# One output transfer, or four on two queues, at the end of a decode kernel

## The chip, the cores and the metric

The kernel runs on one core of a Trainium2 chip. The metric is device time in microseconds (us), from runs on the chip; the lower the better. Beside it there is a profile of one execution, whose span reaches from the first to the last recorded instruction.

## The reference

One decode step of two branches that share a layer norm. Four batch rows of width 576 go in, four rows of 576 come out, in bfloat16.

```
xn  = layernorm(x)                                  # x: [4, 1, 576]
# A: attention over the last 2048 positions of a cache (32 query heads, 16 kv heads, head width 128)
q   = (xn @ wq) as heads
p   = softmax(q . k[window] * 128**-0.5)
a   = (p . v[window]) as one row @ wo
# B: an MLP mixer; with one position its shifted part hs is zero
h2  = gelu(layernorm(xn) @ w3) @ w4
out = x + a + (xn + h2)
```

## The kernel before

Nearly all of the work is reading: 87 MB of cache and weights go once through SBUF. SyncE issues all of these loads from one DMA queue, in the order of the program; each waits until the buffer that it fills has been released. ScalarE's DMA queue carries one transfer, the input `x_bf` (line 98), at the start: four rows of 1152 bytes.

The stages follow each other: the q projection; the scores over eight blocks of K, with the MLP's first product between them; the softmax (line 306 on); then sixteen heads of V, each with its sum, its selection and its part of the output projection; and last the remaining part of `w4`, loaded into `w_end` by five transfers (lines 558 and 559).

In the last stage the result comes together in the PSUM tile `ACC3`. It holds the output cut into four quarter rows of `DQ` = 144 columns: quarter q lies on the partitions from 32q, and of those 32 partitions every eighth (`NB` = 8) holds one of the four batch rows. So 16 partitions, 0, 8, 16 and so on to 120, hold the 16 runs of 144 numbers, 288 bytes each. `quad_out` (line 501) adds the products of `w4` into it, lines 569 to 573 the sums of the two other accumulators, and lines 574 and 575 the last parts of `w4` as their loads land. Then VectorE copies `ACC3` to the SBUF tile `fin` (line 579), and SyncE issues the store (line 580). Its source steps over partitions 0 to 127 by 8; on the side of the output its pattern has three dimensions, quarter, row and column.

After the store the program ends. The closing code, which the profile puts on line 606, is on every engine: SyncE waits for the semaphores of all DMA slots and of the other engines, in five instructions with two semaphores each and one more, and then all engines meet in barriers. Each transfer has one of eight semaphores, which go round; a transfer also waits until the one before it that used the same semaphore has landed. In the list of the closing waits each instruction names two: slots 3 and 2, then 4 and 1, 5 and 0, 6 and VectorE's, 7 and ScalarE's.

Of the kernel before, what the change touches and what calls it, by code (L numbers as in the profile page):

```python
# [20 lines left out]
def kernel(  # L21
# [19 lines left out]
    nc = tc.nc  # L41
    P = 128
# [8 lines left out]
    G = 32  # L51
# [18 lines left out]
    o2 = out.flatten_outer_dims()  # L70
# [289 lines left out]
    NB = B * rep  # L360
# [129 lines left out]
    DQ = D // 4  # L490
# [86 lines left out]

    fin = const.tile([P, DQ], out.dtype)
    nc.vector.tensor_copy(out=fin[:], in_=ACC3[:, 0:DQ])
    nc.sync.dma_start(out=o2.rearrange("b (q n) -> q b n", q=4), in_=fin[0:P:NB, :])  # L580


# [28 lines left out]
```

## Time and profile before

| what | us |
|---|---|
| median of three runs | 213.44 (213.19 to 213.72) |
| span of the profiled execution | 212.0 (212.03 to two places) |
| VectorE busy | 128.2 (60% of the span) |
| TensorE matmul busy | 98.4 (46%) |
| ScalarE busy | 17.4 (8%) |
| read from HBM | 87.17 MB, 411 GB/s over the span |
| the output store, issue on SyncE | 0.69, from 209.20 |

The profiled execution's own time is its span and what lies around it before the first and after the last instruction; the three runs were timed without such a breakdown. SyncE's and ScalarE's DMA-issuing instructions are not counted as busy, but the timeline shows them as SPq and ACTq with the time that issuing took on the engine's sequencer. The transfer itself runs later, on DMA engines. In the DMA view q1 is SyncE's queue and q10 ScalarE's.

### The profile page before, as it was taken

The numbers are of one execution on the slowest core, as the hardware profiler recorded it, in microseconds if no ns is written. First come the engines' busy times: TensorE is split into PE (matmuls) and PEld (weight loads), VectorE is DVE, ScalarE is ACT, GpSimd is POOL, SyncE is SP. The second block draws the span as 40 slices with busy tenths as digits, with TensorE's granted clock in tenths as the row PEclk, the third lists the DMA queues.
The fourth block names the chain that finished last, engine by engine and source line by source line (L and its number), as shares of the span: only waits on it lengthen the run. The fifth ranks groups of instructions, "written<-read, shape, count | busy, mean of one in ns | idle before, by whom it ended". The sixth has DMA issues, their size and how long they took to land. (4 is left out here: it accounts for less than half of the span.)

```text
span 212.0 us, 2539 instructions
## 1 busy us (share of the span) xinstructions
PE 98.4 (46%) x1071; PEld 50.5 (24%) x1071; DVE 128.2 (60%) x225; ACT 17.4 (8%) x35; POOL 1.8 (1%) x8
## 2 busy tenths in 40 slices
PE   1442059429903333423333421968573644555573
PEld 0111027408301011101111101734231321212241
DVE  7812592095349898979699916968475322145240
ACT  0004100000000000000000058730000000000000
POOL 2100000000000000000000000000000000000000
PEclk9999999999999999999999999999787555555555
DMA  7999999999999999999999999999999999999980
GB/s 261 427 457 433 411 442 454 392 420 460 420 420 457 411 445 433 408 451 399 433 427 420 436 415 432 436 423 423 426 430 417 434 415 438 423 427 419 423 356 18
DMA packets 5943, 87.32 MB, mean 412 GB/s; under 512 B 681, under 2 KB 685, under 8 KB 1453
## 3 DMA queue, kind: packets, MB, share of 16 engines
q1 hardware_dynamic: 5924, 87.17, 96.8%
q8 instruction: 8, 0.13, 0.3%
q14 instruction: 3, 0.02, 0.0%
q10 hardware_dynamic: 8, 0.00, 0.0%
HBM read 87.17 MB, written 0.00 MB: 411 GB/s over the span
## 5 line engine op out<-in xcount | busy, mean ns | idle before, releaser
L297 DVE STREAM_TRANSPOSE kt<-k 128x2048 int32<-128x2048 int32 x32 | 71.0, 2278 | 17.5 <-DMA k<-in_A_k_cache_dram 17.5
L304 PE MATMUL S<-kt,qz 128*32 128x512 bf16 x256 | 30.4, 622 | 56.9 <-DVE kt L297 56.9
L384 PE MATMUL O<-v,PZ 128*32 128x512 bf16 x256 | 23.6, 506 | 15.1 <-DMA v<-in_A_v_cache_dram 15.1
L304 PEld LDWEIGHTS <-qz 128*32 128x32 bf16 x256 | 9.5, 127 | 74.0 <-issue 67.5
L413 DVE TENSOR_SCALAR osum<-O,diag 128x128 f32<-128x128 f32 x16 | 5.6, 348 | 28.8 <-PE O L384 28.8
L415 DVE SCALAR_TENSOR_TENSOR osum<-O,diag,osum 128x128 f32<-128x128 f32 x48 | 16.5, 345 | 0.9
L384 PEld LDWEIGHTS <-PZ 128*32 128x32 bf16 x256 | 7.5, 116 | 22.5 <-DMA v<-in_A_v_cache_dram 12.6
L346 PE MATMUL pt<-ident,prs 128*128 128x128 bf16 x64 | 6.5, 287 | 10.1 <-DVE prs L342 10.1
L321 ACT ACTIVATE E<-S,nb 128x256 f32<-128x256 f32 x8 | 4.5, 704 | 69.9 <-DVE nb L318 69.9
L425 PEld LDWEIGHTS OT<-sel,osum 128*128 128x128 f32 x32 | 6.6, 258 | 13.5 <-issue 7.1
L425 PE MATMUL OT<-sel,osum 128*128 128x8 f32 x32 | 8.1, 326 | 3.4 <-DVE osum L415 3.4
L395 PE MATMUL ACC<-wo,onx 128*4 128x288 bf16 x64 | 4.5, 434 | 8.7 <-DVE onx L444 8.7
L346 PEld LDWEIGHTS <-prs 128*128 128x128 bf16 x64 | 5.8, 131 | 11.5 <-ACT prs L340 9.4
L342 DVE TENSOR_SCALAR prs<-E,rdm 128x512 bf16<-128x512 f32 x12 | 7.8, 801 | 0.0
L465 PEld LDWEIGHTS <-w3a 128*128 128x128 bf16 x108 | 6.9, 161 | 1.7 <-issue 1.7
L465 PE MATMUL ACC<-ln2T,w3a 128*128 128x4 bf16 x108 | 7.0, 202 | 0.0
L316 DVE TENSOR_REDUCE mx<-S 128x1 f32<-128x512 f32 x4 | 2.7, 681 | 5.4 <-PE S L304 5.4
L236 PE MATMUL qp<-wq,xnT 128*8 128x512 bf16 x32 | 3.8, 621 | 4.5 <-DMA wq<-in_A_wq_dram 4.5
L567 ACT COPY sums<-ACC 64x288 f32<-64x288 f32 x1 | 0.4, 393 | 64.5 <-PE ACC L395 64.5
L251 DVE CAST q_rows<-qp 128x256 bf16<-128x256 f32 x4 | 1.5, 420 | 5.9 <-PE qp L236 3.9
L340 ACT ACTIVATE prs<-E,rdm 128x512 bf16<-128x512 f32 x4 | 4.9, 1404 | 0.8 <-DVE rdm L328 0.8
L465 PEld LDWEIGHTS <-w3b 128*128 128x128 bf16 x72 | 4.5, 160 | 0.8 <-issue 0.8
(91 smaller groups left out, 68.1 us busy)
## 6 DMA issues: line engine op xcount, KB each, us to landing
v<-in_A_v_cache_dram SPq DMA_DIRECT2D x16, 2048.0 KB, 26.4
k<-in_A_k_cache_dram SPq DMA_DIRECT2D x7, 4096.0 KB, 30.6
wo<-in_A_wo_dram SPq DMA_DIRECT2D x4, 1152.0 KB, 29.8
wq<-in_A_wq_dram SPq DMA_DIRECT2D x2, 2048.0 KB, 12.9
k<-in_A_k_cache_dram SPq DMA_DIRECT2D x2, 2048.0 KB, 25.0
w3a<-in_B_w_dram SPq DMA_DIRECT2D x1, 2304.0 KB, 27.0
w3b<-in_B_w_dram SPq DMA_DIRECT2D x1, 2304.0 KB
w3b<-in_B_w_dram SPq DMA_DIRECT2D x1, 1728.0 KB, 34.6
```

The costliest lines, as they stand in the source:

```text
L297: nc.vector.transpose(out=ap32(kt[e], c0 * 2 * G, [[2 * G, C2 // 2], [1, 2], [2, G]]), in_=ap32(kn, c0 * 4 * G + e * G, [[4 * G, C2 // 2], ...
L304: nc.tensor.matmul(out=S[kq][c:c + 32, :].rearrange("p (c q l) -> p c q l", q=4, l=2), lhsT=qz[:, bp, m, y, :], rhs=kt[e][:, :, 4 * m:4 * ...
L321: nc.scalar.activation(out=E[:, :, g, x:GK:2].rearrange("p (c l) q -> p c q l", l=2), in_=S[g][:, 256 * x:256 * (x + 1)].rearrange("p (c q ...
L340: nc.scalar.mul(out=dst, in_=src, mul=rdm[:, b:b + 1])
L342: nc.vector.tensor_scalar_mul(out=dst, in0=src, scalar1=rdm[:, b:b + 1])
L346: nc.tensor.transpose(out=tp[:, cc, :], in_=pr[:, half * HC + cc, :, :, :].rearrange("p g k b -> p (g k b)"), identity=ident[:])
L384: nc.tensor.matmul(out=bank[G * j:G * j + G, :], lhsT=PZ[:, hp, c0:c0 + NI, :].rearrange("p c m -> p (c m)"), rhs=vn[:, c0:c0 + NI, :].rea ...
L395: nc.tensor.matmul(out=ACCS[half][o0:o0 + B, 0:DH], lhsT=lhsT, rhs=rhs_cols(q * DH, (q + 1) * DH), start=False, stop=False, skip_group_che ...
L413: nc.vector.tensor_scalar_mul(out=osum[:], in0=bank[:, 0:Dh], scalar1=diag[:, 0:1])
L415: nc.vector.scalar_tensor_tensor(out=osum[:], in0=bank[:, i * Dh:(i + 1) * Dh], scalar=diag[:, i:i + 1], in1=osum[:], op0=ALU.mult, op1=AL ...
L425: nc.tensor.matmul(out=OT[:, NB * o:NB * o + NB], lhsT=osum[:], rhs=sel[:], start=True, stop=True, skip_group_check=True)
L465: nc.tensor.matmul(out=gp[:, fc, :], lhsT=lhsT, rhs=rhs, start=False, stop=False, skip_group_check=True)
```

## The change

The one store is replaced by four, one per quarter row, each with a source of four partitions (32q, 32q + 8, 32q + 16, 32q + 24) and a destination of four runs of 144 numbers. Quarters 0 and 2 are issued by SyncE, quarters 1 and 3 by ScalarE.

```
     fin = const.tile([P, DQ], out.dtype)
     nc.vector.tensor_copy(out=fin[:], in_=ACC3[:, 0:DQ])
-    nc.sync.dma_start(out=o2.rearrange("b (q n) -> q b n", q=4), in_=fin[0:P:NB, :])
+    for q in range(4):
+        eng = nc.scalar if q % 2 else nc.sync
+        eng.dma_start(out=o2[:, q * DQ:(q + 1) * DQ], in_=fin[32 * q:32 * q + G:NB, :])
```

`G` is 32 and `NB` is 8. In the built program the instructions of TensorE, VectorE and GpSimd, and their order, are the same as before; SyncE has one DMA instruction more, ScalarE two more, behind all that they had. The transfers take DMA slots 3 (quarter 0) and 5 (quarter 2) on SyncE and 2 (quarter 1) and 4 (quarter 3) on ScalarE, where the single store had slot 2.

## The prediction, made before the run

> **What bounds the kernel now.** I read the chain of waits first, cut to the last 18 us of the span. Its columns are start, length, and what.
>
> ```profile
> 5 pieces in order of time: start us, us, what
> 187.36 20.99 DMA w_end<-in_B_w_dram
> 208.35 0.04 issue
> 208.39 0.45 PE ACC L504 x8
> 208.85 0.02 issue
> 208.87 0.31 DVE fin L579
> ```
>
> The reader sees that up to 208.35 us the last load sets the pace; then eight matmuls and the copy into `fin` follow, and nothing runs beside them that could end later. The page says the same of the whole: the DMA engines stand at 9 tenths in nearly all of the 40 slices. All that the diff touches lies behind 209.2 us, in the last 1.3% of the span, and there every step is exposed. The timeline of the end comes next (start, duration, engine, line, what), together with the instructions of line 606, the end of the program, on SyncE, asked for in two windows (209.9 to 211.02 and 211.0 to 211.3; duration least/median/most in ns, then first and last start).
>
> ```profile
> 205.46 0.39 ACT L567 COPY sums<-ACC 64x288 f32<-64x288 f32 x1 [64.49 <-PE ACC L395]
> 208.87 0.31 DVE L579 CAST fin<-ACC 128x144 bf16<-128x144 f32 x1 [3.05 <-PE ACC L504]
> 209.20 0.69 SPq L580 DMA_DIRECT2D out_dram<-fin  x1
> ...
> L606 SPq EVENT_SEMAPHORE  x1: 1029/1029/1029, 210.0 to 210.0; - x1
> ...
> L606 SPq EVENT_SEMAPHORE  x4: 28/28/28, 211.0 to 211.2; - x4
> ```
>
> ScalarE has been free since 205.85 (205.46 + 0.39). SyncE issues the output for 0.69 us, then waits 1.03 us at line 606, from 209.96 by a window of 10 ns, so until 210.99. Four more waits follow, each alone in a narrow window, at 211.03, 211.09, 211.15 and 211.21: 62 ns apart. When the bytes move is told by the DMA view of 210.45 to 210.65 us, whose 40 slices are 5 ns each:
>
> ```profile
> GB/s 0 0 0 0 0 0 0 0 0 58 0 58 58 0 58 115 0 115 58 0 115 58 0 58 58 0 0 58 0 0 58 0 0 1 0 0 0 0 0 0
> DMA packets 20, 0.00 MB, mean 23 GB/s; under 512 B 20, under 2 KB 20, under 8 KB 20
> ```
>
> The first of the 16 runs starts in the tenth slice, 210.50, and the last packet (a small one, 1 GB/s) in the 34th, 210.62. The 20 packets are 16 runs and four small closing ones, so the transfer is on four DMA engines with five packets each. So the output costs: issue to first packet 1.30 us (210.50 - 209.20), packets 0.12, last packet to end of the wait 0.37 (210.99 - 210.62), and from there to the end of the span 1.04 (212.03 - 210.99).
>
> **The change, part by part.** Removed: one transfer of 16 runs. Added: four of four runs, two behind each other on SyncE and, at the same time, two on ScalarE. The same 4.5 KB and the same 288 B runs move. All four wait for `fin`, ready at 209.19; the other semaphores that they wait for belong to loads whose tiles had been consumed by 204.9. Behind ScalarE's two stands only its closing drain, which has until 211.3 before SyncE joins it: hidden, unless an issue there took over 1 us.
>
> The end is now set by the second transfer of a queue. No transfer of this shape is in the trace, so its price is bounded from these rows (the first two from the start of the program, the others by line: least/median/most in ns):
>
> ```profile
> 0.73 0.55 ACTq L98 DMA_DIRECT2D x_bf<-in_A_x_dram  x1
> 0.74 0.38 SPq L140 DMA_DIRECT2D wq_t<-in_A_wq_dram  x1
> ...
> L122 SPq DMA_DIRECT2D v<-in_A_v_cache_dram x16: 534/541/992, 89.7 to 160.1; - x16
> ...
> L482 SPq DMA_DIRECT2D w_end<-in_B_w_dram x5: 327/328/333, 169.9 to 187.4; - x5
> ```
>
> - First issue: 0.55 us, by the input `x_bf`, the only transfer of four runs. Two rows agree from another side: the loads of line 122, whose pattern has a dimension more than those of line 482, take 0.21 longer (0.534 - 0.328), and the output without that dimension would be 0.69 - 0.21 = 0.48. Ends: 0.33 (line 482) and 0.69 (the output as it is).
> - Gap to the next issue: 0.05 us. Two loads of line 122 took 1.18 us from 89.67 with durations 0.534 and 0.597; so the second of a pair is also 0.06 dearer.
> - Second issue to its first packet: the output's 1.30 less the 0.21 of the dropped dimension, plus 0.06, is 1.15 us. Ends: 0.93 by `x_bf` (its first packet, seen alone in a window on ScalarE's queue, at 1.66) and 1.36 (1.30 + 0.06). `wq_t` has 1.02 (1.76 - 0.74).
> - Packets: two per engine where there were five, 0.12 x 2/5 = 0.05 us. Landing: 0.37 as now.
> - Sum: 209.20 + 0.55 + 0.05 + 1.15 + 0.05 + 0.37 = 211.37, against 210.99: +0.38 us.
> - Tail: SyncE's five waits of line 606 stand in a fixed order in the built program. Before, the output's semaphore is in the first, and four follow at 62 ns. After, the four outputs are in the first, first, second and third, and SyncE's second one is in the third: two follow, so 2 x 0.062 = 0.12 us that stood behind the landing now passes while waiting. If ScalarE's second lands last (second wait), three follow and half of this is kept.
> - Net: +0.38 - 0.12 = +0.26 us, a span of 212.03 + 0.26 = 212.29. Around the span lie 213.44 - 212.03 = 1.41 us by the median of the three runs (the profiled execution's own total is not among them); that gives 213.70.
>
> With all low ends the wait closes at 209.20 + 0.33 + 0.05 + 0.93 + 0.05 + 0.37 = 210.93, a net of -0.18, or 213.26; with all high ends at 209.20 + 0.69 + 0.05 + 1.36 + 0.05 + 0.37 = 211.72, a net of +0.61, or 214.05.
>
> The Trainium skill, on the page DMA: Bandwidth & Descriptors, section Issuing engines are not separate DMA queues, says that starting transfers from several engines saves only the sequencer's issue time, since all run on the same DMA engines. By that rule the second queue saves the two issues that a single queue would add, and the sum stays.
>
> **The rivals.** Main case: as summed, two queues side by side; 213.7, own range 213.25 to 214.1; 0.58.
>
> First rival, slower: SyncE and ScalarE share the step between issue and first packet, so that the four issues pass one by one. The last then starts 3 x 0.60 after the first instead of 0.60, +1.20 us: 214.9. It decides (slower by over 0.64) from +0.38 of those 1.20, a third of it. Against it: `x_bf` and `wq_t` were issued within 0.01 us of each other on the two queues and had their packets after 0.93 and 1.02; for it: the 0.09 between them, and that no two rows show two pairs at once. Chance 0.23; half of it lies under 214.6.
>
> Second rival, slower: a transfer behind another pays for its whole way only when the first has landed. The first takes 209.20 to 210.99, 1.79 us, and the second 1.15 + 0.05 + 0.37 = 1.57: 212.56, net +1.45, 214.9. Against it: line 122's second load was issued 0.58 us after the first and did not wait for its landing. Chance 0.05. The Trainium skill's page DMA: Bandwidth & Descriptors, section Rules for kernel authors, speaks for it and against this change: many small transfers should be made one, since those under 64 KB pay mostly overhead. With the about 2 us that its section Anatomy of one DMA gives as fixed cost (stated there for GpSimd's path) in place of the 1.79, it would be about 215.1.
>
> Third rival, faster: fewer runs and a plainer pattern make the issue as short as line 482's, and the packets come as soon as `x_bf`'s: 213.26 as worked out above. For it: 0.33 is the usual price of a plain pattern on SyncE. Against: those loads use all 16 DMA engines, and the one row of four runs has 0.55. Chance 0.14. Even an issue of no length gives 209.20 + 0.93 + 0.05 + 0.37 = 210.55, net -0.56, less than 0.64: a clear gain needs something that no row shows.
>
> **How the numbers follow.** 0.3% of 213.44 is 0.64 us, about what a measurement of this kernel can tell from no change (its three runs spread over 0.53): faster is under 212.80, slower over 214.08. The main case gives 0.54 no change and 0.04 slower, the first two rivals 0.28 slower, the third 0.10 no change and 0.04 faster. Together: 0.04 faster, 0.64 same, 0.32 slower. The range 213.1 to 214.6 holds the main case, most of the third rival and half of the first, about 0.8.
>
> **What would show it.** In the profile after: SyncE's two issues at 209.2 and 209.8 (all times relative to the end of `fin`), each about 0.5 us; ScalarE's two at the same times. If ScalarE's first starts late or lasts over 0.7, the first rival is at work. Packets in two groups some 0.6 us apart, 16 runs in all; a last group over 1 us behind the first means that a whole transfer was waited for. Line 606 on SyncE: a wait that ends near 211.4, then two or three of 28 ns rather than four. The prediction is wrong in its reason if the span up to `fin` moves by more than 0.3 us, or if the time after the last landing differs from 1.04 - 0.12 by more than 0.1.

## The result, and the profile after

The changed kernel takes 214.41 us (median of 5 runs, 214.18 to 214.47), the kernel before 213.44 (5 runs, 213.19 to 213.83). The ratio is 1.0038, with a 95% interval from 1.0027 to 1.005: slower, by 0.97 us.

The chain of waits of the changed kernel, cut to the same end of the span (start, length, what):

```profile
5 pieces in order of time: start us, us, what
186.95 20.99 DMA w_end<-in_B_w_dram
207.94 0.04 issue
207.98 0.33 PE ACC L504 x8
208.31 0.02 issue
208.33 0.31 DVE fin L579
```

The pieces are those of before, with the same last load of 20.99 us; here `fin` is done at 208.64, before at 209.18. Nothing ahead of the output got longer. The 0.54 us between these two ends is not the change's doing: the instructions ahead of the copy are the same, and in the ten other traces of this case whose work ahead of the copy is that of before, `fin` is done between 208.46 and 208.94, so it was the profiled execution of before that came late. From the end of that copy to the end of the span it is 212.44 - 208.64 = 3.80 us, where it was 212.03 - 209.18 = 2.86: +0.94 us, all of the measured 0.97 within its interval. So the loss lies wholly behind `fin`. The timeline there (start, duration, engine, line, what):

```profile
208.33 0.31 DVE L579 CAST fin<-ACC 128x144 bf16<-128x144 f32 x1 [2.91 <-PE ACC L504]
208.67 1.55 SPq L582 DMA_DIRECT2D out_dram<-fin  x2
208.68 1.31 ACTq L582 DMA_DIRECT2D out_dram<-fin  x2
```

Line 582 by itself gives the single issues (duration least/median/most in ns, first and last start):

```profile
L582 SPq DMA_DIRECT2D out_dram<-fin x2: 746/749/752, 208.7 to 209.5; - x2
L582 ACTq DMA_DIRECT2D out_dram<-fin x2: 602/634/667, 208.7 to 209.4; - x2
```

SyncE needs 1.55 us for two issues, ScalarE 1.31; SyncE's take 0.752 and 0.746, ScalarE's 0.667 and 0.602. A quarter of the output costs SyncE more to issue than the whole output did (0.69). When the bytes move is told by the DMA view of 209.8 to 211.4 us, whose 40 slices are 40 ns each:

```profile
GB/s 0 0 0 0 14 7 7 0 0 0 0 0 0 14 7 7 0 0 0 0 0 0 7 15 7 0 0 0 0 0 0 14 7 7 0 0 0 0 0 0
DMA packets 32, 0.00 MB, mean 3 GB/s; under 512 B 32, under 2 KB 32, under 8 KB 32
...
q1 hardware_dynamic: 16, 0.00, 0.8%
q10 hardware_dynamic: 16, 0.00, 0.8%
```

This is the line to look at longest. There are four groups, and they start in slices 5, 14, 23 and 32: nine slices, 0.36 us, apart, evenly. Two queues that worked side by side would have given two groups. Narrower windows tell the queues apart: ScalarE's, SyncE's, ScalarE's, SyncE's, though both first issues began within 0.01 us of each other. Something takes one store after another, from whichever queue, each for 0.36 us.

The trace also records when a transfer's semaphore is raised, though no view prints it. The semaphore of each of these stores is raised five times, once ahead of its packets and four times behind them. The rise ahead comes 1.12, 1.47, 1.84 and 2.20 us after the end of the copy, about 0.22 us before the store's first packet each time. These rises are 0.36 or 0.37 us apart as well, so the row is formed before a store's own bytes move.

The closing waits on SyncE, from 211.45 us on, asked for by line (duration least/median/most, first and last start):

```profile
L608 SPq EVENT_SEMAPHORE  x3: 28/28/28, 211.5 to 211.6; - x3
```

Five closing waits start between 210.8 and 211.6; the third, for the last landing, starts at 211.50 and ends at 211.52, and two stand behind it, where four did before. From its end to the end of the span it is 0.92 us (212.44 - 211.52) in place of 1.04.

### The profile page after: what moved, and what is told of

It is laid out like the page before. It is cut to its first block, busy times and chain, and to the rows that moved or that the text cites. A ratio compares the mean times of both kernels' runs of the same rounds, so it can differ in the third digit from the quotient of the medians.

```text
span 212.4 us, 2543 instructions
## 1 busy us (share of the span) xinstructions
PE 96.9 (46%) x1071; PEld 49.4 (23%) x1071; DVE 128.2 (60%) x225; ACT 17.3 (8%) x35; POOL 1.8 (1%) x8
```

## The experiments

Three theories were on the table. S: a stage that both queues share takes one transfer after another. Q: each queue has its own pace and only a second transfer on the same queue costs. R: the runs cost, not the transfers. All times below are counted from the end of the copy into `fin`, and each kernel is compared with the kernel before in runs on the same chip. Before, by this count: issue of SyncE from 0.03 to 0.72, first packet 1.32, end of the wait for the landing 1.81, end of the span 2.86.

### Two halves, one on each queue

```
+    HC2 = DQ // 2
+    for c in range(2):
+        eng = nc.scalar if c else nc.sync
+        eng.dma_start(out=o2.rearrange("b (q n) -> q b n", q=4)[:, :, c * HC2:(c + 1) * HC2],
+                      in_=fin[0:P:NB, c * HC2:(c + 1) * HC2])
```

> Two stores of 16 runs each (72 columns, 144 bytes a run), one on SyncE and one on ScalarE, issued at the same moment. Theory S (both queues share a stage that takes one transfer after another, about 0.36 us each, whatever the runs): first packets of the two 0.36 us apart, the later landing 0.36 later than the single store's, 213.44 + 0.36 = 213.8 us. Theory Q (each queue has its own pace and nothing is shared; a second transfer costs only behind another on its own queue): first packets within 0.1 us of each other, 213.4 to 213.5 us. Theory R (the runs cost, as 32 instead of 16): both late, together or apart, by 0.36 each or more, 214.0 us.

213.93 us against 213.62, ratio 1.0014 (1.0005 to 1.0023); span end 3.17, +0.31. The DMA view of 209.8 to 211.4 us, slices of 40 ns:

```profile
GB/s 0 0 0 0 0 25 22 11 0 0 0 0 0 0 25 26 7 0 0 0 0 0 0 0 0 0 0 0 0 0 0 0 0 0 0 0 0 0 0 0
```

Two groups, nine slices apart again: 0.36 us, ScalarE's first (its issue took 0.60, SyncE's 0.70). Each store has 16 runs here and four in the changed kernel, and its packets start over 0.10 us and 0.08, but the spacing is the same, so R falls; the queues are two, and they are not side by side, so Q falls. S gave 0.36 and 213.8.

### The same two halves on one queue

```
-        eng = nc.scalar if c else nc.sync
+        eng = nc.sync
```

> The same two stores of 16 runs, both on SyncE. Theory S and Q alike: the second is issued 0.75 us (0.69 + 0.05) after the first and lands as much later; the closing waits stand as before, so 213.44 + 0.75 = 214.2 us. If the stage of theory S were what sets the pace on one queue as well, the packets would be only 0.36 apart while the issues are 0.75 apart, which can't be; if the issue on SyncE is shorter when ScalarE is silent, 0.55, it is 214.0 us.

214.20 us against 213.62, ratio 1.0031 (1.0021 to 1.0042); span end 3.52, +0.67. The DMA view of 209.6 to 211.2 us, slices of 40 ns:

```profile
GB/s 0 0 0 0 18 25 14 0 0 0 0 0 0 0 0 0 0 0 0 0 0 32 22 4 0 0 0 0 0 0 0 0 0 0 0 0 0 0 0 0
```

On one queue the groups are about 17 slices apart (0.66 us by finer windows), and the second issue, of 0.58 us, starts at 0.78 (the 0.75 us that was expected took it to be as long as the single store's, 0.69). Here the pace is that of the sequencer's issuing, 0.63 from the end of one issue to the end of the next, not of the shared stage. A second queue is worth 0.67 - 0.31 = 0.36 us: it saves issue time and no more, and not all of the 0.63. That agrees with the Trainium skill, page DMA: Bandwidth & Descriptors, section Issuing engines are not separate DMA queues, where a second issuing engine saves only the sequencer's time.

### All four on SyncE

```
     for q in range(4):
-        eng = nc.scalar if q % 2 else nc.sync
+        eng = nc.sync
```

> The four stores of the change, all on SyncE. Theory S: the pace is that of the issue, 0.55 to 0.80 us, the last lands 3 x that after the first, less 0.12 us in the closing waits: 215.0 to 215.7 us, and the time from the end of an issue to its first packet is that of a single store, 0.6 us, for all four. Theory Q: the same pace, 0.80 as SyncE had in the changed kernel, 215.7 us. If SyncE's issue alone takes 0.55 and not 0.75, the rest of the 0.75 was a cost of ScalarE's issuing beside it.

215.18 us against 213.62, ratio 1.008 (1.0067 to 1.0093); span end 4.74, +1.89. Line 581 by itself, and the DMA view of 210.2 to 213.4 us, slices of 80 ns:

```profile
L581 SPq DMA_DIRECT2D out_dram<-fin x4: 578/611/757, 209.0 to 211.1; - x4
```

```profile
GB/s 0 11 4 0 0 0 0 0 0 0 7 7 0 0 0 0 0 0 11 4 0 0 0 0 0 0 11 4 0 0 0 0 0 0 0 0 0 0 0 0
```

The issues take 0.757, 0.644, 0.578 and 0.578, and the first packets follow 1.35, 1.28, 1.23 and 1.23 after each began. So 0.75 is SyncE's own price for the first store of four runs, with ScalarE silent; it isn't caused by the other queue. The second store's packets come 1.28 after its issue began, against 1.59 in the changed kernel. Of those 0.32 us, which ScalarE's stores cost it, 0.10 is a longer issue (0.746 against 0.644) and 0.21 is the wait in the shared stage, from the end of the issue to the first packet (0.85 against 0.63).

### The single store from ScalarE

```
-    nc.sync.dma_start(out=o2.rearrange("b (q n) -> q b n", q=4), in_=fin[0:P:NB, :])
+    nc.scalar.dma_start(out=o2.rearrange("b (q n) -> q b n", q=4), in_=fin[0:P:NB, :])
```

> The single store of before, issued by ScalarE in place of SyncE. Theory S and Q: nothing shared is loaded, 213.4 us, issue 0.6 to 0.75 us, first packet 1.3 us after the issue began. If ScalarE's queue were slower for itself, the first packet would come later than 1.4 us, and part of the changed kernel's loss would be ScalarE's: 213.6 us or more.

213.33 us against 213.62, ratio 0.9988 (0.9979 to 0.9996). ScalarE issues the store in 0.60 us, the first packet comes at 1.28, the span ends at 2.81. ScalarE's queue is no slower than SyncE's, so no part of the loss is its own. It was run once more beside the last experiments:

> The single store on ScalarE once more, beside the other two on this chip. From the traces 0.04 us under before; the runs gave 0.29 (0.9988 with an interval up to 0.9996). If the gain is real it is 0.9985 to 0.9998 again; if it was the scatter of the copy's time, it is 1.000.

213.39 against 213.56, ratio 0.9992 (0.9983 to 1.0001). So it is about 0.1% faster than before, at the edge of what can be told. The trace accounts for 0.03 to 0.04 us of it. Over all runs with a span on record, the span averages 211.40 and 211.45 us (11 runs each) against 211.52 and 211.45 of before (23 and 27), and the rest of the time 1.93 and 1.93 against 2.08 and 2.09. Most of the gain lies outside the span, where no view looks; its cause stays open.

### Sixteen equal rows: what the pattern costs

```
+    nc.sync.dma_start(out=o2.rearrange("b (q n) -> (b q) n", q=4), in_=fin[0:P:NB, :])
```

> One store on SyncE whose output pattern has 16 equal rows instead of four by four, so that it can go to sixteen DMA engines with one run each; the runs land in other places of the output, as quarter and row are exchanged, and the bytes and runs are the same. It measures what the four engines cost. Theory S1 (issue and shared stage are long because a store on four engines has something to do for the twelve that it leaves out): the issue falls from 0.69 to 0.33 to 0.5 us and the first packet comes 0.3 to 0.6 us sooner, 213.0 to 213.2 us. Theory S2 (0.36 us in the stage and 0.7 us of issue are a store's, whatever its engines): issue 0.6 to 0.7, first packet 1.2 to 1.3 us after it began, 213.4 to 213.6 us.

Both kernels of this section put the runs in other places of the output, so they measure the store and cannot replace it. 213.48 us against 213.50, ratio 1.0000 (0.9991 to 1.0008). The 32 packets (16 runs and 16 closing ones) show that sixteen DMA engines are used. The issue is shorter, 0.58, and the first packet comes at 1.28 instead of 1.32, but the last landing at 1.78 instead of 1.79. The third dimension and the four engines, changed together here, are worth 0.11 us of issue and nothing of the time. They are not what makes the store dear: S1 falls.

The same rows in two stores on two queues, against the lines of the two halves:

```
-        eng.dma_start(out=o2.rearrange("b (q n) -> q b n", q=4)[:, :, c * HC2:(c + 1) * HC2],
+        eng.dma_start(out=o2.rearrange("b (q n) -> (b q) n", q=4)[:, c * HC2:(c + 1) * HC2],
                       in_=fin[0:P:NB, c * HC2:(c + 1) * HC2])
```

> The same 16 equal rows in two stores of 72 columns each, one on SyncE and one on ScalarE; again quarter and row are exchanged in the output. Theory S1: the shared stage is nearly empty, first packets of the two queues within 0.15 us of each other and no time lost against the single store of 16 rows. Theory S2: first packets 0.36 us apart as in the two halves of the four-engine pattern, and 0.3 to 0.4 us lost against the single store of 16 rows.

213.76 against 213.50, ratio 1.0011 (1.0002 to 1.0019), span end 3.11 against 2.84 of the single one. The DMA view of 209.6 to 210.4 us, slices of 20 ns:

```profile
GB/s 0 0 0 0 0 0 0 0 36 15 0 29 15 8 8 7 0 0 0 0 0 0 44 8 7 22 15 15 7 0 0 0 0 0 0 0 0 0 0 0
```

The first packets are at 1.24 and 1.52 (by narrower windows), so 0.27 us apart. The shared stage is somewhat shorter for a store on sixteen engines than for one on four (0.27 and 0.36), and it is there for both.

### A load beside the store

```
+    nc.scalar.dma_start(out=fin[0:B, DQ:2 * DQ], in_=x2[:, 0:DQ])
     nc.sync.dma_start(out=o2.rearrange("b (q n) -> q b n", q=4), in_=fin[0:P:NB, 0:DQ])
```

`fin` is twice as wide, and its copy eight columns wider, so that the load waits for it.

> The single store on SyncE as before, and beside it, released by the same copy, a load on ScalarE of four rows of 288 bytes from the input into an unused part of the tile (an addition; the output is the reference's). ScalarE issues it in 0.6 us, so it is through before the store's 0.69. If the shared stage takes every transfer on four engines for 0.36 us, load or store, the store's first packet comes 1.6 to 1.7 us after its issue began instead of 1.30, and the time is 213.8 us. If a load passes quickly, as the input did at the start (packets 0.93 us after its issue began), the store's first packet stays at 1.3 to 1.4 us, 213.4 to 213.5 us.

213.54 us against 213.50, ratio 1.0001 (0.9993 to 1.0010). The timeline (start, duration, engine, line, what), and the DMA view of 209.6 to 210.4 us with slices of 20 ns:

```profile
208.52 0.32 DVE L579 CAST fin<-ACC 128x152 bf16<-128x152 f32 x1 [2.89 <-PE ACC L504]
208.87 0.69 SPq L581 DMA_DIRECT2D out_dram<-fin  x1
208.87 0.26 ACTq L580 DMA_DIRECT2D fin<-in_A_x_dram  x1
```

```profile
GB/s 0 0 0 0 0 0 0 29 0 0 0 0 14 0 0 0 0 14 0 0 0 0 0 0 0 0 0 14 29 86 43 29 29 0 0 0 0 0 0 0
```

This corrects a row that the prediction leaned on. A load of four runs of 288 bytes is issued in 0.26 us, where the store of the same shape takes 0.60 to 0.67 on the same engine; its packets start 0.88 after its issue began, in slice 8, where a store's need 1.3. Nearly all of that difference is the issue: from its end the load needs 0.63 and the store 0.60. Why the input took 0.55 to issue at the start of the program stays open. The store itself starts in slice 28, at 1.32, as if alone. The load was through the shared stage before the store came to it, so whether loads hold it was left open, and three loads were put there.

```
     nc.sync.dma_start(out=o2.rearrange("b (q n) -> q b n", q=4), in_=fin[0:P:NB, 0:DQ])
+    for i in range(3):
+        nc.scalar.dma_start(out=fin[0:B, DQ + 8 * i:DQ + 8 * i + 8], in_=x2[:, 0:8])
```

Here the copy is 24 columns wider than before.

> The single store on SyncE as before, and behind the same copy three loads on ScalarE, four runs of 16 bytes each, into an unused part of the tile (an addition). Issued in about 0.26 us each, they reach the shared stage at about 0.3, 0.6 and 0.9 us after the copy, the store at 0.72. Theory T1 (the stage takes loads and stores alike, 0.36 us each): the store's first packet comes 0.15 to 0.4 us later than the 1.32 us after the copy that it had alone, and the third load waits behind the store. Theory T2 (a load passes the stage in under 0.2 us, and only stores hold it for 0.36): the store's first packet stays within 0.1 us of 1.32, and the third load, if it is behind the store, starts late. The third load lands about 2.0 us after the copy, later than the store's 1.79, so the time may be 0.1 to 0.2 us above before whatever the theory.

213.74 us against 213.56, ratio 1.0009 (1.0000 to 1.0019). The issues of the loads, and the DMA view of 209.5 to 211.1 us, slices of 40 ns:

```profile
L582 ACTq DMA_DIRECT2D fin<-in_A_x_dram x3: 260/303/306, 208.8 to 209.4; - x3
```

```profile
GB/s 0 0 0 1 1 0 0 0 0 0 0 0 1 0 0 7 58 36 14 0 0 0 0 1 0 0 0 0 0 0 0 0 0 0 0 0 0 0 0 0
```

The store's first packet comes at 1.39, 0.06 late; the loads' packets start 0.86, 0.92 and 1.03 after their issues began, and the third is the one whose issue ran beside the end of the store's. That is T2 by its numbers, with a small delay both ways: loads go through the same stage and hold it shortly. How long, these delays do not fix, but the rises of the semaphores do. The first rise of the second load comes at 0.81, that of the store at 1.16 and that of the third load at 1.27. So the store follows a load by 0.36 us, as it follows another store in the changed kernel, and the load follows the store by 0.10. The third load's rise is also ahead of the store's packets (1.39): it did not wait until the store had moved its bytes.

### The closing waits

Two kernels put the single store on ScalarE and move its semaphore to SyncE's fifth closing wait by cutting five loads in two: five of K in the first, the four of wo and the early one of w4 in the second.

```
-        cuts = 2 if last else 1
+        cuts = 2 if last or 2 <= 4 * bp + kq <= 6 else 1
```

> The single store on ScalarE, and five loads of K in two halves each, so that the store's semaphore is the one in SyncE's fifth and last closing wait instead of the first. If the waits behind the landing cost 62 ns each, the time from the store's landing to the end is 0.25 us shorter than 1.04, and with ScalarE's shorter issue the time is 213.44 - 0.25 - 0.1 = 213.1 us, against 213.33 of the single store on ScalarE. If cutting the loads costs the stream something, the copy into the last tile comes later and the total is 213.3 or more, with the closing part shorter all the same.

```
+        for a in range(0, XR * D, XR * D // 2):
+            nc.sync.dma_start(out=wo_row[:, a:a + XR * D // 2], in_=wo_src[:, g2, a:a + XR * D // 2])
...
-            w4 = load_w4(w3_b[:, JR * F:JR * F + 12 * D].rearrange("p (i n) -> p i n", n=D), 0, 0, 0, (12,))
+            w4 = load_w4(w3_b[:, JR * F:JR * F + 12 * D].rearrange("p (i n) -> p i n", n=D), 0, 0, 0, (6, 6))
```

> Again the single store on ScalarE with its semaphore in SyncE's fifth closing wait, but the five transfers that move it there come from cutting the four loads of wo and the early load of w4 in two, and K is loaded as before. If the closing waits are worth what the trace of the first such kernel showed (2.58 us from the copy to the end instead of 2.86) and only the cutting of K took it back, the time is 0.2 to 0.3 us under before, 0.9987. If the copy comes as late as there, any cutting of the stream costs as much, and the time is that of before.

The span ends at 2.58 and 2.59 after the copy, 0.23 and 0.24 sooner than with the single store on ScalarE and four waits behind its landing (2.81 and 2.83): about 60 ns a wait, as their spacing of 62 ns said. The times show little of it: 213.50 against 213.50, ratio 1.0002 (0.9993 to 1.0010), and 213.36 against 213.56, ratio 0.9991 (0.9983 to 1.0000). Averaged over 11 runs each, the span is 211.66 against 211.45, and 211.56 against 211.45. With an end that is shorter than before's by 0.28 and 0.26 (2.86 - 2.58, 2.86 - 2.59, rounded), the copy must come 0.49 and 0.37 us later on average. By the span, cutting five loads costs the stream more than the closing code gives back, whichever five they are; where in the stream stays open. By the whole time it costs about as much as it gives: the second kernel and the single store on ScalarE, run on the same chip, take 213.36 and 213.39, and the time outside the span was shorter again, 1.81 against 1.93.

## Why the prediction was right, and where it was not

The range held the time and the direction was right, but the likeliest case was not what happened. It put 213.7 and no change, from a net of +0.26; the trace has +0.94. The main case's own range, up to 214.1, and the sum of all its high ends, 214.05, were both passed. What held 214.41 is the room up to 214.6 that was left for the first rival.

Right: that nothing ahead of the copy changes; that the second transfer of SyncE sets the end; the gap (0.05, measured 0.05); the packets (0.05, measured 0.08); the landing (0.37, measured 0.38); the tail, where two closing waits instead of four follow (0.92, measured 0.92); ScalarE's drain, hidden.

Wrong, first: "Second issue to its first packet", 1.15 us, measured 1.59. The main case had the queues side by side, and this step holds 0.44 of the 0.68 that the forecast lacked. In its place the runs showed one stage for both queues: 0.36 us a store in the changed kernel and in the two halves. It can be checked in one line: ScalarE's first packet is at 1.34, and 1.34 + 3 x 0.36 = 2.42 is where SyncE's second store has its first, by the trace. With ScalarE silent the same step took 1.28 (four on SyncE), so 0.32 of the 0.44 comes from ScalarE's stores, 0.21 as the wait in the shared stage and 0.10 as a longer issue, and the rest from an estimate that was too low. Without those 0.32 the loss behind `fin` would have been about 0.62 (an estimate, 0.94 - 0.32). So some two thirds of it is the price of a second store on SyncE's own queue, and one third comes from ScalarE's stores.

Wrong, second: "First issue: 0.55 us, by the input". Measured 0.752, another 0.20. The row was the nearest by its shape, four runs, but it was a load. Taking off 0.21 for the pattern's third dimension was also wrong for a store: the plain pattern of four runs took 0.75, not 0.48. So was adding 0.06 for the second of a pair: SyncE's second store was issued in 0.746 after 0.752, and in 0.644 after 0.757 with ScalarE silent. The first issue and the second's way to its first packet both came out above the high ends that were set for them, 0.69 and 1.36.

So the first rival had the mechanism, at 0.23, and an oversized price: it let the four issues pass one by one at 0.60, +1.20 over the main case. The stage takes 0.36 a store, and the issues overlap it; the result lies 0.68 over the main case's net, and at most 0.32 of that comes from ScalarE's stores. Its own point, from +0.38 on, was passed, and the measured 0.97 is over the 0.64 that it named. The evidence held against it, that `x_bf` and `wq_t` started on two queues with 0.09 us between their packets, was about loads, which pass quickly.

Three of the signs that were to tell the cases apart misled. ScalarE's first issue neither started late nor lasted over 0.7 (0.667), though the first rival was at work. The last group of packets came 1.08 us behind the first, which was to mean that a whole transfer is waited for; it was three steps of 0.36. And `fin` was done 0.54 us earlier than in the profile of before, over the limit of 0.3, with nothing changed ahead of it: that limit was narrower than the scatter between executions (208.46 to 208.94 in the ten other traces, 209.18 before).

The second rival falls: on one queue a second store is issued from 0.78 to 1.36 (two halves on SyncE), while the first lands at 1.78, and its first packet comes 0.63 us after the end of its issue, about as with the single store (0.60). It waits for its issue and not for the landing; from the first packets of one store to those of the next it is 0.66 us there, and 0.73 in four on SyncE. The rule that was cited beside it, from the Trainium skill's page DMA: Bandwidth & Descriptors, section Rules for kernel authors, that small transfers should be made one, is borne out in its direction: 0.31 for two and 0.94 for four on two queues, 0.67 and 1.89 on one. The third rival falls with the issue of 0.75.

One number of the sum's frame was off without effect: the 1.41 us around the span. The profiled execution of before had a long span. In other runs its span averages 211.45 to 211.52 with 2.06 to 2.09 around it, and the changed kernel's five runs have 212.32 and 2.06. The net was taken from differences, so this moved nothing.

## What to carry to other kernels

The store that ends this program is a row of steps, 2.86 us from the last copy to the end for 4.5 KB, and cutting it added to them: 0.36 us between one store and the next even on a second queue, 0.62 to 0.73 on the same one. To price an added transfer take a row of the same direction; a load of the same shape was issued in 0.26 us where the store took 0.60 or more. And when packets can be seen, look at their spacing across queues: even steps that follow neither queue's issue are the mark of something shared.

## What was not expected of the hardware

- Stores from SyncE and ScalarE pass one after another, 0.36 us each on four DMA engines, with 4 or 16 runs alike, and 0.27 on sixteen. A load behind a store followed it by 0.10. What the stage is made of, these runs do not tell.
- The same store was issued in 0.69 us by SyncE and in 0.60 by ScalarE.
- On SyncE four plain stores in a row were issued in 0.757, 0.644, 0.578 and 0.578 us, and the store of 16 runs with one dimension more in 0.69. Why the first plain one is the dearest stays open.
- With the store on ScalarE, 0.15 us of the time outside the span went away (1.93 against 2.08 and 2.09 on average). It was 1.86 with four stores on SyncE, so the issuing engine alone does not explain it.
